# A pre-norm attention and MLP block on one core: key and value loads enter the DMA queue one attention step later, and two low parts go to GpSimd

## The chip, the cores and the metric

The kernel runs on one core of a Trainium2 chip. The metric is the device time of one execution in microseconds, the median of several runs. TensorE is PE in the profile, VectorE DVE, ScalarE ACT, GpSimd POOL, and SyncE SP. Almost all DMAs are issued by SP, so one queue, in one order, carries the loads, the stores and the transposes done by DMA.

## The reference, cut to what matters

```python
# x: (1, 2048, 512) float32; 32 heads of 16; window of 8 positions, 2 apart
def attention(x, wqkv, wo):
    q, k, v = split_heads(x @ wqkv)
    idx = pos[:, None] - 2 * arange(8)[None, :]          # masked where negative
    logits = einsum("bhsd,bhswd->bhsw", q, k[idx]) * Dh ** -0.5
    o = einsum("bhsw,bhswd->bhsd", softmax(where(idx >= 0, logits, -1e9)), v[idx])
    return merge_heads(o) @ wo

def mlp(x, w1, b1, w2, b2):                              # hidden width 1792
    return relu(x @ w1 + b1) ** 2 @ w2 + b2

h  = x + attention(layernorm(x), wqkv, wo)
h2 = h + mlp(layernorm(h), w1, b1, w2, b2)
```

## The kernel before, in words

All matrix products are made from float32 values split in two: a *high part* is the value rounded to a shorter float32 format by ACT (`hi`, L152), and a *low part* is the value minus its high part, a subtraction on DVE or POOL (`lo`, L155). Each product is three matmul passes, high by high, low by high, high by low. TensorE so does 2,414 matmuls, and the program's order is written so that they follow each other without a gap.

The 2,048 rows are 16 tiles of 128 positions. Tiles of even and of odd positions are kept apart, so the window with its stride of 2 becomes 8 neighbouring rows. The projections `q`, `k`, `v` are written to a DRAM buffer `qkv_d` and read back in windows.

*Attention* runs beside the matmuls, on DVE and POOL, and takes no matmul. It is a generator (`attention`) that hands out one *step* at a time. `dots(j)` multiplies a window of keys `k` with queries in PSUM, `qp` (L340, result `pr`); a reduction (L374) makes logits of it. `weigh(j)` multiplies a window of values `v` with the weights (L351, result `pr` too); POOL then adds the eight rows of the window in three instructions (`add_up`, L408), into `o`. Tiles `k`, `v` and `q` have two buffers each and `pr` three. Each step loads the key or value window of the step two ahead of it: `load_k`, and with every second one `load_q`, at the end of `dots`; `load_v` at the end of `weigh` (DMAs L247 and L260). The window so loaded goes into the buffer that the multiplication just emitted reads, so the DMA has to wait for that multiplication, and SP, which issues in order, waits with it. ACT copies `q` to PSUM (L268).

The order of everything is written by *slots*. A slot is one block of matmuls. What goes with a slot is put in lists: `due` (run at its end, before attention), `amid`, and `late` (after attention). `end_slot` runs `due`, then `pump`, which draws attention steps until their estimated DVE time has caught up with TensorE's, then `amid` and `late`. In the first pass over the MLP (4 tiles; u = 0) each slot also loads a block of `w2` (`raw`, L1057), splits it (ACT cast to `big_h`, low part `big_l` by POOL, every third by DVE), and stores the low part to DRAM for later passes (`stash`, `w2l_d`, L1086). The results `o` are turned to the layout that TensorE needs through 16-bit planes: ACT splits (`pl`, L621), a DMA transposes (L625), ACT joins (L630), then ACT rounds to the high part (`oh`, or `ohl` for every fourth tile) and DVE makes the low part. The product with `wo` reads these.

For the last four tiles the first MLP product is made from 7 instead of 8 block products, with sums of blocks of its input. `split_last` prepares them for tiles 14 and 15: `tr` is the joined tile `pl`; `hs_[1]` and `ls_[1]` are the high and low part of its second half; `sm[1]` and `sm[2]` are sums (in `s`), whose high and low parts follow. All of its subtractions and additions are on DVE.

Of the kernel before, what the change touches and what calls it, by code (L numbers as in the profile page):

```python
# [58 lines left out]
def block_kernel(ctx, tc, x, wqkv, wo, w1, b1, w2, b2, out):  # L59
    nc = tc.nc  # L60
# [75 lines left out]
    def dve(t):  # L136
        now["dve"] += t
# [16 lines left out]
    def lo(eng, dst, src, h):  # L154
        eng.tensor_tensor(out=dst, in0=src, in1=h, op=ALU.subtract)  # L155
# [86 lines left out]
    def load_window(n, j, c, name):  # L242
        s, g0, ng = items[n]
        u, b, e, i0 = where(s)
        t = att.tile([P, R + W - 1, GC], F32, name=name)
        sl = (R if u == 0 else RI) + W - 1
        nc.sync.dma_start(t[:, :sl], chain(e, g0 + j, c, CH // 2 * b + 1 + i0,  # L247
                                           [[R * GC, P], [GC, sl], [1, GC]]))
        return t
# [6 lines left out]
    def load_q(n, j):  # L256
        s, g0, ng = items[n]
        u, b, e, i0 = where(s)
        q = att.tile([P, 2, RI, GC], F32, name="q")
        nc.sync.dma_start(q.rearrange("p j i c -> p j (i c)"),  # L260
                          chain(e, g0 + j, 0, PAD + CH // 2 * b + i0,
                                [[R * GC, P], [CS, 2], [1, RI * GC]]))
        return q
# [7 lines left out]
    def attention():  # L271

        N = len(items)

        def ready(n):
            gps = [(items[n][1] + j) // 2 for j in range(0, items[n][2], 2)] if n < N else []
            return n < N and all((items[n][0] // RI, gp) in stored and gp in padded
                                 for gp in gps)

        steps = [(n, j) for n in range(N) for j in range(items[n][2])]  # L280
        ks, vs, qs, qps, ex = {}, {}, {}, {}, {}


        logits = psum.tile([P, 2, D // 2], F32, name="ex", tag="ex")

        def ahead(n, j, by):
            i = steps.index((n, j)) + by
            return steps[i] if i < len(steps) else (N, 0)

        def load_k(n, j):  # L290
            if ready(n) and (n, j) not in ks:
                ks[n, j] = ks[n - 1, j] if items[n][0] == 1 else load_window(n, j, 1, "k")
                if j % 2 == 0:
                    qs[n, j] = load_q(n, j)

        def load_v(n, j):
            if ready(n) and (n, j) not in vs:
                vs[n, j] = vs[n - 1, j] if items[n][0] == 1 else load_window(n, j, 2, "v")

        def next_q(n, j):  # L300
            if (n, j) in qs:
                qps[n, j] = q_to_psum(qs.pop((n, j)))

        while not ready(0):
            yield None
        for j in range(2):
            load_k(0, j)
        for j in range(2):
            load_v(0, j)
        for _ in range(DELAY):  # L310
            yield None
        for n in range(N + 1):

            new, old = n < N, n > 0
            while new and not ready(n):
                yield None
            ng = ng1 = 0
            if new:
                s, g0, ng = items[n]
                u, b, e, i0 = where(s)  # L320
                HG = ng * GH
                for j in range(2):
                    load_k(n, j)
                if (n, 0) not in qps:
                    next_q(n, 0)
                lf = logits[:, n % 2, :RI * W * HG].rearrange("p (i w h) -> p i w h", i=RI, w=W)
                mx = small.tile([P, RI, HG], F32, name="mx")
            if old:
                s1, g1, ng1 = items[n - 1]
                e1 = ex.pop(n - 1)  # L330
                sm = small.tile([P, RI, ng1 * GH], F32, name="sm")
                if s1 not in o_t:
                    o_t[s1] = att.tile([P, RI, D], F32, name="o", bufs=3)

            def dots(j):
                kwin = window(ks[n, j], s, [1, GC])
                pr = att.tile([P, RI, W, GH, DH], F32, name="pr", bufs=3)
                if j % 2 == 0:
                    qps["now"] = qps.pop((n, j))
                nc.vector.tensor_tensor(  # L340
                    out=pr.rearrange("p i w h d -> p i w (h d)"),
                    in0=qps["now"][:, j % 2].unsqueeze(2).to_broadcast([P, RI, W, GC]),
                    in1=kwin, op=ALU.mult)
                load_k(*ahead(n, j, 2))
                return pr

            def weigh(j):
                load_v(n - 1, j)
                vwin = window(vs[n - 1, j], s1, [DH, GH], [1, DH])
                p2 = att.tile([P, RI, W, GH, DH], F32, name="pr", bufs=3)  # L350
                nc.vector.tensor_tensor(  # L351
                    out=p2, in1=vwin, op=ALU.mult,
                    in0=e1[:, :, :, j * GH:(j + 1) * GH].unsqueeze(4).to_broadcast(
                        [P, RI, W, GH, DH]))
                sums.append((p2, o_t[s1], (g1 + j) * GC, s1))
                load_v(*ahead(n - 1, j, 2))

            for j in range(max(ng, ng1)):
                if j < ng:
                    pr = dots(j)  # L360
                    yield 1.22
                if old and j == 0:
                    nc.vector.tensor_reduce(out=sm, in_=e1.rearrange("p i w h -> p i h w"),
                                            axis=X, op=ALU.add)
                    yield 0.23 + 0.035 * ng1
                if 0 < j < ng1 or 0 < j == ng1 < ng:
                    if j == 1:
                        nc.vector.tensor_tensor(
                            out=e1, in0=e1, op=ALU.mult,
                            in1=sm.unsqueeze(2).to_broadcast([P, RI, W, ng1 * GH]))  # L370
                    weigh(j - 1)
                    yield 1.55 if j == 1 else 1.26
                if j < ng:
                    nc.vector.tensor_reduce(out=lf[:, :, :, j * GH:(j + 1) * GH], in_=pr, axis=X,  # L374
                                            op=ALU.add)
                    yield 1.22
                    if j % 2:
                        next_q(*((n, j + 1) if j + 1 < ng else (n + 1, 0)))
                if old and j == 0:
                    nc.vector.reciprocal(sm, sm)  # L380
                    yield 0.26
            if new and b == 0:
                nc.vector.tensor_tensor(
                    out=lf, in0=lf, op=ALU.add,
                    in1=mask[:, i0:i0 + RI].unsqueeze(3).to_broadcast([P, RI, W, HG]))
                yield 0.16 + 0.07 * ng
            if old and ng1 >= ng:
                weigh(ng1 - 1)
                yield 1.26
            if new:  # L390
                nc.vector.tensor_reduce(out=mx, in_=lf.rearrange("p i w h -> p i h w"), axis=X,
                                        op=ALU.max)
                nc.vector.tensor_tensor(out=lf, in0=lf, op=ALU.subtract,
                                        in1=mx.unsqueeze(2).to_broadcast([P, RI, W, HG]))
                ex[n] = lf
                yield 0.42 + 0.15 * ng
                nc.scalar.activation(lf, lf, AF.Exp, scale=DH ** -0.5)

    sums = []

    def add_up(p2, o, c0, s):
        w = W // 2
# [9 lines left out]
    def pump(until=None):  # L414

        while (done[until] < G) if until is not None else (now["dve"] < now["pe"]):
            if until is None and now["dve"] > now["pe"] - HALF:
                run(amid)
            todo = sums[:]
            sums.clear()  # L420
            t = next(stream, "end")
            for a in todo:
                add_up(*a)
            if t == "end":
                now["dve"] = 1e9
                return
            if t is None:
                now["dve"] = max(now["dve"], now["pe"])
                return
            dve(t * SLOW[min(now['sub'] + 1, 2)])  # L430
# [306 lines left out]
    def split_last(i, tr):  # L737
        hs_, ls_ = [a[:, :, i] for a in hh], [a[:, :, i] for a in hl]
# [4 lines left out]
        j = i - RI  # L743
# [12 lines left out]
        hi(hs_[1], tr[:, 2:])  # L756
        tt(out=sm[1], in0=tr[:, 2:], in1=a21, op=add)
        tt(out=sm[2], in0=sm[1], in1=tr0[:, :2], op=sub)
        lo(nc.vector, ls_[1], tr[:, 2:], hs_[1])
        hi(a_h[2][:, :, j], sm[2])  # L760
        lo(nc.vector, a_l[2][:, :, j], sm[2], a_h[2][:, :, j])
        if not j:
# [331 lines left out]
    for u in range(R - 1):  # L1094
# [11 lines left out]
        for i in js:  # L1106
            t = R * (u + 1) + i
            if not end:
                a = i // 2 if u == 2 else 0
# [148 lines left out]
```

## Time and profile before

| | |
|---|---|
| median of 3 runs | 504.54 us (503.73 to 505.6) |
| the profiled execution | 504.29 us, of which the span from first to last instruction is 502.5 us |
| granted TensorE clock | 1.000 |
| TensorE matmuls busy | 496.0 us, 99% of the span |
| DVE, ACT, POOL busy | 381.6 us (76%), 301.6 us (60%), 353.9 us (70%) |
| DMA | 103.15 MB, mean 205 GB/s |
| chain that ended last | PE 80%, DVE 5%, POOL 4%, ACT 4%, DMA 3%, issue 3% |

TensorE's busy time is nearly the whole span, so what counts is where it stops and what it then waits for. The other engines are idle a quarter to a third of the time, and a delay on one of them costs nothing until a matmul waits for it. The chain of waits follows the work that ended last back to its start.

### The profile page before, as it was taken

Reading aid. Unit: us, or ns where it says so; the run is one execution under the profiler, and the core shown is the slowest. Engines: PE = TensorE matmul, PEld = TensorE weight load, DVE = VectorE, ACT = ScalarE, POOL = GpSimd, SP = SyncE. Lnnn points to the kernel's source line nnn. Section 1 sums busy time; section 2 is a strip of 40 time slices with the busy share of each in tenths; the row PEclk is TensorE's granted clock in tenths of the full one; section 3 lists DMA queues with packets and bytes.
Section 4 is the critical chain, followed back from the end, with each engine's and each line's share of the span. In section 5 each row is a group of like instructions: output and inputs, shape, how many; then the busy total and the mean of one; then the engine's idle time right before and its main releaser. Section 6 shows DMA issues by size and latency. Waiting matters only on the chain.

```text
span 502.5 us, 7519 instructions
## 1 busy us (share of the span) xinstructions
PE 496.0 (99%) x2414; PEld 420.5 (84%) x2414; DVE 381.6 (76%) x524; ACT 301.6 (60%) x540; POOL 353.9 (70%) x430
## 2 busy tenths in 40 slices
PE   8999999999999999999999999999999999999997
PEld 7999888888888888887888888888888888998986
DVE  6479899988989899988879998888974155833233
ACT  4635687668446758368564555755554958766541
POOL 5714898885685999869777877769799363786610
PEclk9999999999999999999999999999999999999999
DMA  9679979889698989589676756966654566355112
GB/s 280 184 221 243 294 234 316 254 291 282 201 226 255 299 283 257 182 239 224 195 253 209 211 150 193 232 213 237 211 160 66 128 165 188 112 162 167 64 42 86
DMA packets 111472, 103.15 MB, mean 205 GB/s; under 512 B 31560, under 2 KB 79944, under 8 KB 111432
## 3 DMA queue, kind: packets, MB, share of 16 engines
q1 hardware_dynamic: 110488, 102.14, 69.5%
q10 hardware_dynamic: 944, 0.52, 0.3%
q8 instruction: 19, 0.31, 0.3%
q14 instruction: 21, 0.17, 0.1%
HBM read 72.65 MB, written 24.25 MB: 193 GB/s over the span
## 4 chain that ended last, share of the span: by engine, by line
PE 80%; DVE 5%; POOL 4%; ACT 4%; DMA 3%; issue 3%; ACTq 0%; SPq 0%; DVEq 0%; POOLq 0%
PE mm L228 41%; PE acc L899 23%; PE wo L228 8%; PE mm L822 7%; PE tr L201 2%; POOL pr L408 1%; DVE pr L351 1%; DMA raw<-in_B_w_dram 1%; DMA o<-pl 1%; DMA wraw<-in_A_wqkv_dram 1%; POOL rl L155 1%; DVE ex L374 1%; DVE pr L340 1%; ACT pl L621 1%; ACT big_h L152 1%
## 5 line engine op out<-in xcount | busy, mean ns | idle before, releaser
L408 POOL TENSOR_TENSOR pr<-pr 128x512 f32<-128x512 f32 (+1 forms) x128 | 134.2, 1049 | 36.7 <-DVE pr L351 31.4
L228 PE MATMUL mm<-big_l,w_h 128*128 128x512 f32 x336 | 88.5, 390 | 0.0
L351 DVE TENSOR_TENSOR pr<-ex,v 128x1024 f32<-128x1024 f32 x64 | 78.0, 1220 | 12.2 <-POOL o L408 8.0
L340 DVE TENSOR_TENSOR pr<-qp,k 128x1024 f32<-128x1024 f32 x64 | 76.8, 1200 | 11.7 <-ACT qp L268 7.9
L374 DVE TENSOR_REDUCE ex<-pr 128x64 f32<-128x1024 f32 x64 | 78.5, 1226 | 2.0
L228 PEld LDWEIGHTS mm<-big_l,w_h 128*128 128x128 f32 x336 | 62.9, 188 | 13.5 <-ACT r L875 0.2
L155 POOL TENSOR_TENSOR rl<-r,rh 128x512 fp32r<-128x512 f32 x42 | 54.7, 1306 | 25.5 <-ACT rh L152 25.4
L228 PE MATMUL mm<-big_l,xh 128*128 128x512 f32 (+1 forms) x208 | 55.8, 378 | 0.0
L228 PE MATMUL mm<-big_h,xh 128*128 128x512 f32 (+1 forms) x208 | 53.6, 378 | 0.9 <-ACT xh L152 0.8
L228 PE MATMUL mm<-big_h,xl 128*128 128x512 f32 (+1 forms) x208 | 52.6, 374 | 0.0
L899 PE MATMUL acc<-big_h,rh 128*128 128x512 f32 x190 | 52.0, 391 | 0.0
L899 PE MATMUL acc<-big_l,rh 128*128 128x512 f32 x190 | 52.0, 390 | 0.0
L899 PE MATMUL acc<-big_h,rl 128*128 128x512 f32 x190 | 51.7, 389 | 0.0
L228 PE MATMUL mm<-big_l,w_l 128*128 128x512 f32 x168 | 44.9, 389 | 0.0
L228 PEld LDWEIGHTS mm<-big_h,xh 128*128 128x128 f32 x208 | 37.7, 188 | 7.8 <-ACT xh L152 2.0
L228 PEld LDWEIGHTS mm<-big_h,xl 128*128 128x128 f32 x208 | 38.2, 188 | 6.0 <-DVE xl L155 0.2
L899 PEld LDWEIGHTS acc<-big_h,rl 128*128 128x128 f32 x190 | 35.7, 188 | 7.4
L899 PEld LDWEIGHTS acc<-big_l,rh 128*128 128x128 f32 x190 | 35.6, 188 | 7.5
L228 PEld LDWEIGHTS mm<-big_l,xh 128*128 128x128 f32 x208 | 37.5, 188 | 4.9
L899 PEld LDWEIGHTS acc<-big_h,rh 128*128 128x128 f32 x190 | 35.0, 188 | 6.7
L875 ACT ACTIVATE r<-mm,b_sb 128x512 f32<-128x512 f32 x42 | 28.7, 684 | 14.0 <-PE mm L228 13.1
L228 PEld LDWEIGHTS mm<-big_l,w_l 128*128 128x128 f32 x168 | 31.5, 188 | 6.6
(160 smaller groups left out, 910.6 us busy)
## 6 DMA issues: line engine op xcount, KB each, us to landing
k<-qkv_d SPq DMA_DIRECT2D x48, 288.0 KB, 3.6
v<-qkv_d SPq DMA_DIRECT2D x48, 288.0 KB, 3.7
qkv_d<-y SPq DMA_DIRECT2D x18, 512.0 KB, 4.0
big_l<-w2l_d SPq DMA_DIRECT2D x24, 256.0 KB, 3.2
xt<-in_A_x_dram SPq DMA_DIRECT2D x16, 256.0 KB, 4.3
q<-qkv_d SPq DMA_DIRECT2D x32, 128.0 KB, 3.7
h<-in_A_x_dram SPq DMA_DIRECT2D x16, 256.0 KB, 3.6
h_d<-h SPq DMA_DIRECT2D x16, 256.0 KB, 2.8
```

Source lines behind the costliest of these rows:

```text
L152: nc.scalar.copy(dst, src)
L155: eng.tensor_tensor(out=dst, in0=src, in1=h, op=ALU.subtract)
L201: nc.tensor.transpose(tr[:, k, :], src[:, k * P:(k + 1) * P], ident)
L228: nc.tensor.matmul(ps, l(k), r(k), start=(n == 0), stop=(n == 3 * KB - 1))
L340: nc.vector.tensor_tensor(out=pr.rearrange("p i w h d -> p i w (h d)"), in0=qps["now"][:, j % 2].unsqueeze(2).to_broadcast([P, RI, W, GC]) ...
L351: nc.vector.tensor_tensor(out=p2, in1=vwin, op=ALU.mult, in0=e1[:, :, :, j * GH:(j + 1) * GH].unsqueeze(4).to_broadcast([P, RI, W, GH, DH]))
L374: nc.vector.tensor_reduce(out=lf[:, :, :, j * GH:(j + 1) * GH], in_=pr, axis=X, op=ALU.add)
L408: nc.gpsimd.tensor_tensor(out=dst, in0=p2[:, :, :w], in1=p2[:, :, w:2 * w], op=ALU.add)
L621: nc.scalar.copy(two_planes(planes[key][1]), halves_of(src))
L822: nc.tensor.matmul(ps, sta[y][:, k], mov[x][:, k], start=(first and q == 0), stop=(last and q == len(terms) - 1), skip_group_check=True)
L875: nc.scalar.activation(r, ps, AF.Relu, bias=b1_sb[:, f:f + 1])
L899: nc.tensor.matmul(acc[j], l[:, j * P:(j + 1) * P], w[f], start=(first and n < len(js)), stop=(last and n >= len(terms) - len(js)))
```

## The change

The loads of a step are no longer issued at its end. They are put in a list, `loads`, and `pump` issues what is in the list right before it draws the next step. Within one `pump` call nothing but an `amid` chore can come between. But the last step of a `pump` leaves its loads in the list until the next `pump`: by then the `amid` and `late` chores of this slot and the `due` chores of the next have put their DMAs into the queue. Of the 112 loads of keys and values 35 change places with later DMAs, and 9 of the 32 loads of queries with them; at most six DMAs come ahead of one load. No instruction of PE or ACT changes place.

The second part moves the low part `ls_[1]` in `split_last` from DVE to POOL, for tiles 14 and 15.

```diff
@@ dots(j)
                     in1=kwin, op=ALU.mult)
-                load_k(*ahead(n, j, 2))
+                loads.append((load_k, ahead(n, j, 2)))
                 return pr
@@ weigh(j)
                 sums.append((p2, o_t[s1], (g1 + j) * GC, s1))
-                load_v(*ahead(n - 1, j, 2))
+                loads.append((load_v, ahead(n - 1, j, 2)))
@@
-    sums = []
+    sums, loads = [], []
@@ pump(until)
                 run(amid)
             todo = sums[:]
             sums.clear()
+            ready_loads = loads[:]
+            loads.clear()
+            for fn, a in ready_loads:
+                fn(*a)
             t = next(stream, "end")
@@ split_last(i, tr)
         tt(out=sm[2], in0=sm[1], in1=tr0[:, :2], op=sub)
-        lo(nc.vector, ls_[1], tr[:, 2:], hs_[1])
+        lo(nc.gpsimd, ls_[1], tr[:, 2:], hs_[1])
         hi(a_h[2][:, :, j], sm[2])
```

The first place is SP's queue in the first MLP pass, around the transpose of the first `o` tile of that pass. `raw` is a block of `w2`, `w2l_d` the store of a low part. Before:

```order
L247 DMA v<-qkv_d 128x576
L247 DMA k<-qkv_d 128x576
L260 DMA q<-qkv_d 128x2x128
L625 DMA_TRANSPOSE o<-pl 128x8x128
L1057 DMA raw_2307<-in_B_w_dram 128x512
L1086 DMA w2l_d<-big_l 128x512
L247 DMA k<-qkv_d 128x576
```

The same place of SP's queue after the change (lines below the diff are four higher):

```order
L247 DMA v<-qkv_d 128x576 x2
L629 DMA_TRANSPOSE o<-pl 128x8x128
L1061 DMA raw_2303<-in_B_w_dram 128x512
L1090 DMA w2l_d<-big_l 128x512
L247 DMA k<-qkv_d 128x576
L260 DMA q<-qkv_d 128x2x128
L247 DMA k<-qkv_d 128x576
```

A load of keys and one of queries moved behind the transpose, the block of `w2` and the store. The store waits for a low part of POOL.

The second place is DVE in `split_last` for tiles 14 and 15, before:

```order
L757 TENSOR_TENSOR s<-pl 128x2x128
L758 TENSOR_TENSOR s<-s,pl 128x2x128
L155 TENSOR_TENSOR big_l<-pl,big_l 128x2x128
L155 TENSOR_TENSOR big_l<-s,big_l 128x2x128
L757 TENSOR_TENSOR s<-pl 128x2x128
L758 TENSOR_TENSOR s<-s,pl 128x2x128
L155 TENSOR_TENSOR big_l<-pl,big_l 128x2x128
L155 TENSOR_TENSOR big_l<-s,big_l 128x2x128
L766 TENSOR_TENSOR s<-pl 128x2x128
```

And POOL at that time after the change:

```order
L683 TENSOR_TENSOR h<-h,b_sb 128x512
L155 TENSOR_TENSOR tl<-traw,th 128x512 x2
L155 TENSOR_TENSOR rl<-r,rh 128x512
L155 TENSOR_TENSOR big_l<-pl,big_l 128x2x128 x2
L155 TENSOR_TENSOR tl<-traw,th 128x512
L854 TENSOR_TENSOR r<-u,p 128x256
```

The two rows `big_l<-pl,big_l` left DVE's list, and stand on POOL behind `rl` and ahead of the next `tl`.

## The prediction

> **What bounds the kernel now.** I read the busy times by stretch first, since TensorE is busy for 496.0 of 502.5 us and the question is where the rest lies. Columns: stretch, its length, then busy time (and instructions) of PE, PEld (weight loads), DVE, ACT, POOL, the clock, the DMA share and GB/s.
>
> ```profile
> 17.00:227.00 210.00, 210.00 (x997) 178.10 (x996) 186.66 (x245) 130.24 (x261) 157.36 (x200) 1.00 0.84 251
> 227.00:230.00 3.00, 2.49 (x12) 1.74 (x11) 1.73 (x2) 2.97 (x5) 2.67 (x4) 1.00 1.02 231
> 230.00:426.00 196.00, 196.00 (x880) 162.29 (x879) 149.91 (x202) 118.38 (x187) 144.26 (x165) 1.00 0.68 190
> 426.00:432.00 6.00, 5.53 (x43) 5.00 (x42) 5.58 (x13) 4.16 (x8) 2.56 (x3) 1.00 0.06 17
> ```
>
> From 17 to 426 us, which is where all the moved loads lie, TensorE misses 0.51 us, in one place. Between 426 and 432 it misses 0.47, in the place of the second edit. The timeline of PE shows both (start, length, engine, line, operation; in brackets the idle time before and who ended it):
>
> ```profile
> 227.34 1.07 PE L899 MATMUL acc<-big_h,rl 128*128 128x512 f32 x4
> 228.91 1.20 PE L228 MATMUL wo<-wo_h,ohl 128*128 128x512 f32 x4 [0.51 <-ACT ohl L152]
> ...
> 426.64 0.40 PE L822 MATMUL mm<-wo_h,tl 128*128 128x256 f32 x2
> 427.50 0.51 PE L822 MATMUL mm<-wo_l,th 128*128 128x256 f32 x2 [0.47 <-DVE wo_l L155]
> ```
>
> The chain of waits says what the first stop hangs on (start, length, what):
>
> ```profile
> 202.43 1.30 POOL pr L408
> ...
> 218.33 1.05 ACT pl L621
> ...
> 228.24 0.63 ACT ohl L152
> 228.91 3.01 PE wo L228 x12
> 231.93 2.72 PE mm L228 x12
> ```
>
> POOL's sums from 202.43 give the `o` tile that ACT splits at 218.33, and ACT's `ohl` at 228.24 lets TensorE go on. What starts POOL later at 202.43 makes the stop longer.
>
> **The most that can be gained.** Twelve matmuls take 2.72 us in an even run, 0.227 each. The four from 227.34 would make room for the next at 228.25, so 0.66 us is lost by 228.91; the first twelve then take 3.01, another 0.29. The stop is worth 0.95 us in all, 0.44 over its idle time. The second, with the same surplus as an estimate, is worth 0.47 + 0.44 = 0.91. If both go, the sum is 1.86 us, 0.37%. A change of 0.5%, 2.5 us, is about what a measurement of this kernel can tell from none, so the change cannot make a difference on the fast side that a measurement shows; on the slow side nothing limits it so.
>
> **Edit 1, the loads.** No instruction is added or removed; 44 loads stand later in SP's queue and the DMAs that they let pass stand earlier. DVE's use of values and keys, and ACT's of the blocks of `w2` (idle time before each, and who ended it):
>
> ```profile
> L351 DVE TENSOR_TENSOR pr<-ex,v 128x1024 f32<-128x1024 f32 x64 | 78.0, 1220 | 12.2 <-POOL o L408 8.0 <-DMA v<-qkv_d 1.9
> L340 DVE TENSOR_TENSOR pr<-qp,k 128x1024 f32<-128x1024 f32 x64 | 76.8, 1200 | 11.7 <-ACT qp L268 7.9 <-POOL o L408 3.6
> L152 ACT CAST big_h<-raw 128x512 fp32r<-128x512 f32 x12 | 7.4, 616 | 2.4 <-DMA raw<-in_B_w_dram 2.4
> ```
>
> Loads hardly make DVE wait now: 1.9 us in 64 steps for values, none for keys. So most delays have cover, the time between landing and use. What passes ahead has little to give by itself either: ACT waited 2.4 us in all for the blocks of `w2`, while TensorE ran on. The transposes are the exception that could help the stop at 228.91. I look at the place where cover is thinnest, SP's queue at 190 us with what ACT and DVE do there, and POOL (its rows last):
>
> ```profile
> 190.86 0.32 SPq L247 DMA_DIRECT2D k<-qkv_d  x1
> 191.27 0.39 SPq L260 DMA_DIRECT2D q<-qkv_d  x1
> 191.75 1.24 SPq L625 DMA_TRANSPOSE o<-pl  x1
> 193.08 0.53 SPq L1057 DMA_DIRECT2D raw<-in_B_w_dram  x1
> 195.26 0.32 SPq L1086 DMA_DIRECT2D w2l_d<-big_l  x1
> 196.17 1.17 ACT L630 COPY pl<-o 128x1024 uint16<-128x1024 uint16 x1 [0.24 <-DMA o<-pl]
> 198.36 1.22 DVE L340 TENSOR_TENSOR pr<-qp,k 128x1024 f32<-128x1024 f32 x1
> 199.50 1.72 DVE L155 TENSOR_TENSOR ol<-pl,oh 128x512 fp32r<-128x512 f32 x1
> 193.93 1.29 POOL L155 TENSOR_TENSOR big_l<-raw,big_h 128x512 fp32r<-128x512 f32 x1
> 199.37 1.30 POOL L155 TENSOR_TENSOR rl<-r,rh 128x512 fp32r<-128x512 f32 x1
> ```
>
> *The gain side.* The transpose no longer stands behind the key load, which SP could only issue at 190.86 when DVE had freed its buffer, nor behind the query load; it goes 0.9 us earlier at the least (191.75 - 190.86), and more by what SP waited before 190.86. ACT waited 0.24 us for it at 196.17. Nothing follows from this: the `ol` that DVE makes of it at 199.50 already takes 1.72 us, because it ends only after POOL's `rl` (199.37 + 1.30 = 200.67). Gain taken: 0. Its far end is the whole first stop, 0.95.
>
> *The loss side.* The store `w2l_d` at 195.26 waits for POOL's low part (193.93 + 1.29 = 195.22), and the moved loads wait with it: keys at about 195.7, queries at about 196.1 (0.41 apart as now), instead of 190.86 and 191.27, 4.8 us later. DVE uses both at 198.36, through ACT's copy of the queries. How long a query load takes is shown once by a wait and once by the page's median (SP and ACT rows, then the page's row, last number: us to landing):
>
> ```profile
> 176.22 0.43 SPq L260 DMA_DIRECT2D q<-qkv_d  x1
> 178.97 0.38 ACT L268 COPY qp<-q 128x256 f32<-128x256 f32 x1 [3.72 <-DMA q<-qkv_d]
> q<-qkv_d SPq DMA_DIRECT2D x32, 128.0 KB, 3.7
> ```
>
> By the first, 2.75 us from issue to use, the copy starts at 198.9 and DVE's L340 at 199.3; by the second, at 199.8 and 200.2. L340 takes 1.22. In the first case `ol` is ready to run at 200.5, still under POOL's `rl`, and ends at 201.2 as before: POOL's start at 202.43 does not move, price 0. In the second `ol` starts at about 201.4, after `rl`. Without that wait it takes 0.69 at most (1.72 less the 1.17 from 199.50 to 200.67 leaves 0.55), so it ends at 202.1 instead of 201.22: 0.9 later, and with it POOL's chain, ACT and the stop at 228.91. So edit 1 costs 0 to 0.9. I take 0.1: the first case is the nearer row, a query load issued right behind a key load in the same stretch, and it leaves the path unmoved.
>
> Other places by the same reading: loads go behind such stores in the slots before this one too. From the issue at 190.86 to the use at 198.36 are 7.5 us, of which a load needs 2.75 to 3.7 by the rows above, so a delay up to 3.8 us is covered where the distances are like these. From 230 to 426 TensorE never stops. I take 0 there; a delay of DVE that reaches a matmul would cost its length.
>
> **Edit 2, two low parts by POOL.** DVE loses two instructions of 0.42 us. The question is what DVE was doing around them (DVE's rows, then ACT's, then POOL's):
>
> ```profile
> 421.28 1.10 DVE L757 TENSOR_TENSOR s<-pl 128x256 f32<-128x256 f32 x1 [3.52 <-POOL tl L155]
> 422.49 0.43 DVE L758 TENSOR_TENSOR s<-s,pl 128x256 f32<-128x256 f32 x1
> 422.83 0.42 DVE L155 TENSOR_TENSOR big_l<-pl,big_l 128x256 fp32r<-128x256 f32 x1
> 423.39 0.43 DVE L155 TENSOR_TENSOR big_l<-s,big_l 128x256 fp32r<-128x256 f32 x1
> 422.95 0.41 ACT L152 CAST big_l<-s 128x256 fp32r<-128x256 f32 x1 [0.36 <-DVE s L758]
> 424.64 0.41 ACT L152 CAST big_l<-s 128x256 fp32r<-128x256 f32 x1 [0.98 <-DVE s L758]
> 420.81 1.29 POOL L155 TENSOR_TENSOR rl<-r,rh 128x512 fp32r<-128x512 f32 x1
> 431.21 0.72 POOL L850 TENSOR_TENSOR r<-u,p 128x256 f32<-128x256 f32 x1
> ```
>
> The low part at 422.83 lies between L758, which ends at 422.92, and the low part of `s` at 423.39. That one needs ACT's cast, which waits for L758 and runs from 422.95 to 423.36. So the moved instruction fills a hole: without it DVE stands idle until 423.39 all the same. The second pair is alike, ACT's cast at 424.64 again waiting for DVE. Removing 0.84 us of DVE work therefore gains 0, and the stop at 427.50, which ends with a later DVE instruction of this chain, does not shrink. A gain is excluded by this as long as ACT's cast waits for L758.
>
> What it adds are two POOL instructions. POOL is free from 422.10 (420.81 + 1.29), and by the row at 431.21 a tensor of 128x256 takes it 0.72. But the row at 421.28 shows what the two engines do to each other: an instruction of DVE that takes 0.42 or 0.43 everywhere else here took 1.10, and ended 0.28 after POOL's `rl` did. Both inputs are in SBUF. If POOL's first low part starts when L758 ends, 422.92, it ends at 423.64. DVE's instruction of 423.39 then ends at 423.92 instead of 423.82, a loss of 0.1. The second low part has its input while DVE runs the next L757 and L758. If POOL comes in between these, L758 and all behind it are 0.72 later; if it comes behind them, into the hole of the next cast, the loss is as small as the first. Edit 2 so costs 0.1 + 0.1 to 0.1 + 0.72, 0.2 to 0.8, with 0 as the far end if the engines do not meet. I take 0.5, the middle, since I see no row that says which engine goes first. TensorE's stop at 427.50 grows by that; behind it TensorE is the bound until the end, so it shows in the time.
>
> [...]
>
> **The sum.** The profiled execution took 504.29 us, 0.25 below the median of the runs. 504.29 + 0.1 + 0.5 = 504.9.
>
> **The rivals.** *Late queries (slower).* The loads behind a store wait for POOL, DVE waits for the loads, POOL waits for DVE, and the next store waits for POOL. It decides when the copy of the queries starts later than 199.0, the last moment at which `ol` still ends under POOL's `rl`. At 0.9 for one such place, three places in a row (the stores of the slots at 172 to 196 us) give 2.7, and with edit 2 507.5. For it: POOL's row at 193.93 does set the store at 195.26, and a delay of 4.8 us is more than the cover of 3.8. Against it: 1.9 us of waiting for loads in all of the run before, so cover of several us at most places.
>
> *Both stops go (faster).* The earlier transpose and the queue that is no longer blocked let DVE run ahead, POOL reaches 202.43 a us sooner, and POOL's low parts fall in DVE's holes: 504.29 - 1.86 = 502.4. For it: the transpose feeds `ol` at 199.50, and DVE reaches the `pr` of 202.43 only behind that. Against it: ACT waited just 0.24 us for one, and edit 2 frees no DVE time that anyone waits for.
>
> *Nothing shows.* All moved loads have cover, what passes ahead has no one waiting for it, and POOL's low parts meet no DVE instruction: 504.3.
>
> **How the numbers follow.** Forecast 0.55; nothing shows 0.25; both stops go 0.12; late queries 0.08. The range goes from 503.0, part of the way to the case of both stops gone, to 506.6, which holds 0.9 and 0.8 together with some of the late queries; outside are most of the 0.08 and about 0.1 below. Faster by over 0.5% (under 502.0) is beyond the ceiling of the gain, and has only the spread of the runs for it: 0.04. Slower by over 0.5% (over 507.1) is the case of late queries, with a little left to the spread: 0.07. Within 0.5%: 0.89.
>
> **What would show it.** Right: PE idle by about 0.5 before `ohl` near 228.9, and by about 1.0 before `wo_l` near 428; DVE's rows near 422 to 425 with one of 0.7 to 1.1 us beside POOL's new ones; ACT's copy of queries near 198.9 ended by a DMA; the transpose issued before 190.9. Wrong: a stop of TensorE in a stretch that has none now; `ol` near 200 ending later than 201.5; the stop near 427.5 gone or smaller, which would mean that the freed DVE time was on the path after all.

## The result, and the profile after

The changed kernel took 508.38 us (median of 7 runs, 506.82 to 509.54) against 504.54 before (7 runs, 503.73 to 505.6). The ratio is 1.0069, 95% interval 1.0047 to 1.0092: slower, by 3.8 us in the medians. The forecast was 504.9 with a range to 506.6. The profiled execution took 507.16 us, its span is 505.3.

The page of the profile after, its head and busy times:

```profile
span 505.3 us, 7505 instructions
...
PE 496.3 (98%) x2414; PEld 420.5 (83%) x2414; DVE 380.3 (75%) x522; ACT 301.4 (60%) x540; POOL 355.9 (70%) x432
```

TensorE does the same work in the same time; only the span is longer. The busy times by stretch (columns as in the prediction), cut at the same two places, which now lie 2 us later:

```profile
17.00:228.00 211.00, 210.86 (x999) 178.50 (x998) 183.83 (x244) 129.36 (x259) 156.73 (x200) 1.00 0.83 250
228.00:232.00 4.00, 1.93 (x9) 1.26 (x9) 2.71 (x3) 3.90 (x7) 3.76 (x4) 1.00 0.91 217
232.00:428.00 196.00, 196.00 (x879) 162.29 (x878) 149.32 (x198) 118.20 (x188) 146.16 (x168) 1.00 0.66 189
428.00:434.00 6.00, 5.12 (x40) 4.60 (x38) 5.52 (x14) 3.70 (x8) 1.91 (x2) 1.00 0.10 29
```

TensorE misses 2.07 us in the second stretch, where it missed 0.51, and 0.88 in the last, where it missed 0.47. Its timeline shows both stops, with the same releasers as before:

```profile
228.05 1.07 PE L903 MATMUL acc<-big_h,rl 128*128 128x512 f32 x4
231.19 1.19 PE L228 MATMUL wo<-wo_h,ohl 128*128 128x512 f32 x4 [2.07 <-ACT ohl L152]
...
430.15 0.50 PE L826 MATMUL mm<-wo_l,th 128*128 128x256 f32 x2 [0.88 <-DVE wo_l L155]
```

The first stop is 1.56 us longer (2.07 - 0.51), the second 0.41 (0.88 - 0.47). Another 0.14 is missed ahead of 228 us. These are 2.1 of the span's 2.8; the rest is a few tenths at the start, near 63 us and at the end.

To see why `ohl` is late, follow the trace from the first MLP pass on. SP's issues, ACT, POOL and DVE of the changed kernel (start, length, engine, line, operation; in brackets the idle time before and who ended it):

```profile
173.95 0.43 SPq L599 DMA_DIRECT2D h<-in_A_x_dram  x1
174.47 2.45 SPq L247 DMA_DIRECT2D v<-qkv_d  x1
177.02 0.38 SPq L247 DMA_DIRECT2D k<-qkv_d  x1
177.45 0.42 SPq L260 DMA_DIRECT2D q<-qkv_d  x1
180.67 0.38 ACT L268 COPY qp<-q 128x256 f32<-128x256 f32 x1 [4.41 <-DMA q<-qkv_d]
182.94 0.62 ACT L152 CAST rh<-r 128x512 fp32r<-128x512 f32 x1
183.64 1.30 POOL L155 TENSOR_TENSOR rl<-r,rh 128x512 fp32r<-128x512 f32 x1 [1.11 <-ACT rh L152]
183.70 1.78 DVE L155 TENSOR_TENSOR big_l<-raw,big_h 128x512 fp32r<-128x512 f32 x1
195.67 1.30 POOL L155 TENSOR_TENSOR big_l<-raw,big_h 128x512 fp32r<-128x512 f32 x1
196.99 0.32 SPq L1090 DMA_DIRECT2D w2l_d<-big_l  x1
197.84 0.46 SPq L260 DMA_DIRECT2D q<-qkv_d  x1
201.15 0.38 ACT L268 COPY qp<-q 128x256 f32<-128x256 f32 x1 [0.39 <-DMA q<-qkv_d]
204.60 2.10 POOL L408 TENSOR_TENSOR pr<-pr 128x512 f32<-128x512 f32 x2 [1.87 <-DVE pr L351]
```

And the same two low parts, DVE's `big_l` and POOL's `rl`, in the kernel before:

```profile
181.65 0.83 DVE L155 TENSOR_TENSOR big_l<-raw,big_h 128x512 fp32r<-128x512 f32 x1
181.93 1.71 POOL L155 TENSOR_TENSOR rl<-r,rh 128x512 fp32r<-128x512 f32 x1
```

At 174 us a value load, which before was issued at the end of the step before this one, comes behind the load of `h` and right ahead of the key and query loads that the next `dots` needs. The copy of the queries starts at 180.67 against 178.97. In both traces ACT runs `big_h`, `r`, `r` and `rh` behind the copy, in this order, and the `rh` is late by as much as the copy (182.94 against 181.23, 1.71 us; the copy 1.70), and POOL, which had no idle time ahead of this `rl`, now waits 1.11 us. That `rl` then runs beside DVE's `big_l`. The two met in the kernel before as well, but there DVE's came first (181.65) and took 0.83 us, and POOL's took 1.71. Now POOL's comes first (183.64 against 183.70) and takes 1.30, and DVE's takes 1.78. From there all is late: `big_l` of POOL at 195.67 (before 193.93), the store at 196.99 (195.26), the queries behind it at 197.84 instead of 191.27, their copy at 201.15 (197.95), POOL's sums at 204.60 (202.43), and at the end `ohl`.

### The profile page after: what moved, and what is told of

Same layout as the page of the kernel before. It is cut to its first block, busy times and chain, and to the rows that moved or that the text cites. A ratio compares the mean times of both kernels' runs of the same rounds, so it can differ in the third digit from the quotient of the medians.

```text
span 505.3 us, 7505 instructions
## 1 busy us (share of the span) xinstructions
PE 496.3 (98%) x2414; PEld 420.5 (83%) x2414; DVE 380.3 (75%) x522; ACT 301.4 (60%) x540; POOL 355.9 (70%) x432
## 4 chain that ended last, share of the span: by engine, by line
PE 80%; DVE 2%; ACT 2%; POOL 2%; issue 1%; POOLq 0%; DVEq 0%; ACTq 0%
PE mm L228 36%; PE acc L903 26%; PE wo L228 9%; PE mm L826 7%; PE tr L201 2%; ACT pl L625 1%; POOL tl L155 1%; POOL pr L408 0%; DVE s L761 0%; PE half L926 0%; POOL rl L155 0%; DVE s L762 0%; ACT r L880 0%; POOL h L683 0%; DVE pr L351 0%
## 5 line engine op out<-in xcount | busy, mean ns | idle before, releaser
L340 DVE TENSOR_TENSOR pr<-qp,k 128x1024 f32<-128x1024 f32 x64 | 76.9, 1201 | 13.6 <-ACT qp L268 10.4
```

The lines of the kernel that those rows point to most:

```text
L340: nc.vector.tensor_tensor(out=pr.rearrange("p i w h d -> p i w (h d)"), in0=qps["now"][:, j % 2].unsqueeze(2).to_broadcast([P, RI, W, GC]) ...
```

## Experiments

Each kernel ran beside the kernel before on the same chip, whose medians were 504.0 to 504.58 us; ratios are to it.

### The two edits apart

The loads alone: the change, with

```diff
-        lo(nc.gpsimd, ls_[1], tr[:, 2:], hs_[1])
+        lo(nc.vector, ls_[1], tr[:, 2:], hs_[1])
```

> Only the deferred loads; the low part ls_[1] is on DVE again. Theory A (queries that are loaded behind a store that waits for POOL reach ACT late, ACT's queue delays POOL's rl and DVE's multiplication, POOL's sums start later, and TensorE waits longer for ohl near 230 us): the stop there stays at about 2.1 us against 0.5 before, the stop near 428 is 0.5 again, the span is 504.1 to 504.9 against 502.5, the ratio to before 1.003 to 1.005. Theory B (the loss comes of the two low parts on POOL): ratio 1.000, both stops as before. Theory C (the loss is the lower granted clock of some runs, not the stop): span of runs at clock 1.0 as before, and 2 us more where the clock is 0.996.

The low parts alone: the kernel before, with that line the other way round.

> Only the two low parts on POOL; the loads are issued at once as before. Theory A: the stop near 230 us is 0.5 as before, the one near 427 us 0.9 against 0.5, the span 502.9, the ratio 1.0008 (within the spread). Theory B: the ratio is that of the whole change, 1.005 to 1.007. Theory C: ratio 1.000 to 1.001, with a clock of 1.0 in all runs.

The loads alone: 506.84 us, ratio 1.0053 (1.0030 to 1.0075). The low parts alone: 504.78, 1.0005 (0.9994 to 1.0016). TensorE's waits in the first and then in the second (what, us in total, times, longest):

```profile
PE wo L228 <- ACT ohl L152: 2.1, 1, 2.1
...
PE mm L826 <- DVE wo_l L155: 0.5, 1, 0.5
```

```profile
PE mm L822 <- DVE wo_l L155: 0.9, 1, 0.9
```

Each edit lengthens its own stop and not the other's. In the profile of the low parts alone the first stop, 0.51 before, isn't there at all, though nothing ahead of it was changed: so it varies by half a microsecond from one execution to the next. Theory B is out. Of theory C something is left: in 5 of 9 runs the first kernel's clock was 0.992 to 0.997, and four runs at 0.999 or 1.0 had a median span of 504.1 (the kernel before beside it 502.8), the five others 506.4. That is taken up below.

### Which of the loads

The loads alone, but not in the first MLP pass:

```diff
-                loads.append((load_k, ahead(n, j, 2)))
+                if now["sub"] == 0:
+                    load_k(*ahead(n, j, 2))
+                else:
+                    loads.append((load_k, ahead(n, j, 2)))
```

(and the same for `load_v`).

> The deferred loads alone, but in the first pass over the MLP (about 170 to 230 us), where slots also load and store blocks of w2, the loads are issued at once as before. Theory A: the stop near 229 us is 0.5 again, no stop elsewhere, the ratio 0.999 to 1.001. If loads deferred elsewhere cost too: a stop at another place and a ratio of 1.002 or above.

Ratio 1.0000 (0.9992 to 1.0009). The loads deferred everywhere else cost nothing that this interval of 0.1% shows. The next two split the pass by time: from here on the first place is 174 to 177 us, and the second is 190 to 198 us, the part of SP's queue that the section on the change lists. They have other slots in that condition: `88 <= now["slot"] < 94` leaves only the second place deferred, `94 <= now["slot"] < 102` only the first.

> The deferred loads alone, but in the first MLP pass only from the slot of the second place on (the keys and queries behind the transpose and the store at 190 to 198 us); in the six slots ahead of it the loads are issued at once as before. By the prediction's own bounds for this place, 0 to 0.9 us: the copy of the queries starts at 198.9 to 199.8 and the stop near 229 us is 0.5 to 1.4, the ratio 1.000 to 1.002. If this place makes the whole loss by itself: the copy at 201, the stop 2, the ratio 1.004 to 1.006.

> The complement: in the first MLP pass the loads are deferred in its first six slots alone (the loads behind the store and the load of h at 174 to 177 us), and issued at once from the second place on. Theory A: the chain of POOL is 0.8 to 1.1 us late at 196 us, the keys and queries of the second place are in time, the stop is 1.0 to 1.4, the ratio 1.001 to 1.002; with the other run's surplus it adds up to the 1.6 us of both. By the prediction, which took 0 here: the stop 0.5, the ratio 1.000.

The second place alone: 1.0020 (1.0005 to 1.0034), the first alone 1.0061 (1.0040 to 1.0083). Rows of ACT, POOL and DVE, then TensorE's stop, with the second place alone:

```profile
179.24 0.38 ACT L268 COPY qp<-q 128x256 f32<-128x256 f32 x1 [4.90 <-DMA q<-qkv_d]
182.20 1.63 POOL L155 TENSOR_TENSOR rl<-r,rh 128x512 fp32r<-128x512 f32 x1
181.92 0.75 DVE L155 TENSOR_TENSOR big_l<-raw,big_h 128x512 fp32r<-128x512 f32 x1
199.20 0.38 ACT L268 COPY qp<-q 128x256 f32<-128x256 f32 x1 [1.31 <-DMA q<-qkv_d]
202.65 2.12 POOL L414 TENSOR_TENSOR pr<-pr 128x512 f32<-128x512 f32 x2 [1.78 <-DVE pr L354]
229.13 1.21 PE L228 MATMUL wo<-wo_h,ohl 128*128 128x512 f32 x4 [0.57 <-ACT ohl L152]
```

And with the first place alone:

```profile
174.78 1.49 SPq L260 DMA_DIRECT2D q<-qkv_d  x1
179.77 0.38 ACT L268 COPY qp<-q 128x256 f32<-128x256 f32 x1 [4.23 <-DMA q<-qkv_d]
182.74 1.30 POOL L155 TENSOR_TENSOR rl<-r,rh 128x512 fp32r<-128x512 f32 x1 [0.80 <-ACT rh L152]
181.97 1.22 DVE L354 TENSOR_TENSOR pr<-ex,v 128x1024 f32<-128x1024 f32 x1 [0.57 <-POOL o L414]
183.12 1.47 DVE L155 TENSOR_TENSOR big_l<-raw,big_h 128x512 fp32r<-128x512 f32 x1
199.77 0.37 ACT L268 COPY qp<-q 128x256 f32<-128x256 f32 x1
203.61 2.11 POOL L414 TENSOR_TENSOR pr<-pr 128x512 f32<-128x512 f32 x2 [1.76 <-DVE pr L354]
230.23 1.42 PE L228 MATMUL wo<-wo_h,ohl 128*128 128x512 f32 x4 [1.87 <-ACT ohl L152]
```

In its profile the second place behaves as the prediction priced it: the copy at 199.20, between its 198.9 and 199.8, POOL 0.2 later than before, the stop 0.57. That execution, 504.38 us, is the second fastest of its twelve; the median is 505.61, 1.4 above the kernel before, and where the others lost it no run shows. The first place, which the prediction took at 0, makes nearly the whole stop by itself. There a copy that is 0.5 us later (179.77 against 179.24) makes `rl` 0.5 later, and DVE's L354 waits another 0.57 for POOL; DVE's `big_l`, so 1.2 later, is now behind POOL's `rl` and takes 1.47 instead of 0.75, and DVE's next L340 starts 1.9 later (185.64 against 183.72). The expectation, a stop of 1.0 to 1.4 and a ratio of 1.001 to 1.002, was too low. The times do not add up: the first place alone costs about as much as both. The stops nearly do: 0.06 and 1.36 above the 0.51 of before are 1.4, and both together gave 1.56.

The query load of this kernel was issued earlier than before (174.78 against 176.22; the issue itself lasts to 176.27) and used later. A value load of 288 KB more stood ahead of it and of its key load. In the packed traces the last landing mark of the query load comes 0.35 to 0.44 us behind that of the key load ahead of it in all four kernels: 178.89 and 178.53 before, 179.69 and 179.33 here, 180.60 and 180.16 with the whole change, 181.27 and 180.92 with the values alone. So here the query load lands right behind the load ahead of it, whenever it was issued.

Three more kernels cut the chain at other points. Queries issued at once, only keys and values deferred (`load_k` no longer asks for those that were):

```diff
+        def ask_q(n, j):
+            if ready(n) and j % 2 == 0 and (n, j) not in asked:
+                asked.add((n, j))
+                qs[n, j] = load_q(n, j)
...
+                ask_q(*ahead(n, j, 2))
                 loads.append((load_k, ahead(n, j, 2)))
```

> Only the deferred loads, and of these only keys and values: the queries are issued at the end of the step as before (the first of the three late ones still comes behind a store, since its step is drawn at another moment). Theory A: the two later queries are ahead of their stores, so the feedback is broken after the first place; the copy that starts at 201.15 in the changed kernel starts at 198.5 to 200, the stop near 230 us is 0.5 to 1.3, the span 502.5 to 503.7, the ratio 1.000 to 1.0025. A variant, A2 (the late keys and values hold DVE as well): the stop stays at 2 us and the ratio at 1.003 to 1.005.

Only values deferred:

```diff
-                loads.append((load_k, ahead(n, j, 2)))
+                load_k(*ahead(n, j, 2))
```

> Of the deferred loads only those of values; keys and queries are issued at the end of the step as before, and the low part ls_[1] is on DVE. At the first place (174 to 177 us) the key and query loads still follow a value load and a load of h, but at the second (190 to 198) they are ahead of the transpose and the store again. Theory A: what makes the stop long is the second place's keys and queries; the copy of the queries near 198 us no longer waits for a DMA, the stop near 229 us is 0.5 to 1.0, no clock below 0.998, the ratio 1.000 to 1.002. If late values do it: the stop stays at 2, the ratio at 1.004 or above.

All deferred, and the store of the low part one slot later:

```diff
-            at(1, stash, f)
+            at(2, stash, f)
```

> All loads deferred as in the change, the low part ls_[1] on DVE, and the store of the low part of w2 put into the queue one slot later, so that its low part is made long before and SP need not wait for POOL in front of the loads. Theory A: the stop near 230 us falls from 2.1 to 0.5 to 0.9, the span is 502.5 to 503, the ratio 1.000 to 1.001. If what delays the loads is not the store's wait but the number of DMAs ahead of them (the block of w2, the transpose): the stop stays at 1.5 to 2 us, the ratio at 1.003 to 1.005.

Ratios 1.0017 (1.0006 to 1.0029), 1.0012 (1.0000 to 1.0024) and 1.0022 (1.0010 to 1.0034), with a stop of 1.1, 1.3 and 1.1 us. Each takes away roughly 60 to 80% of the loss of the loads alone and none all of it; the later store came out between its two expectations. The late queries, the late keys and the store in front of both are links of one chain; which of the loads at the first place weighs most, these runs don't settle: with the values alone the copy waited 7.24 us there, and the stop was still only 1.3.

### What a stop costs

The kernel before, with ACT's join and cast of that one tile repeated ahead of `ohl`, once each:

```diff
+        for _ in range(1 if t == 6 else 0):
+            nc.scalar.copy(...)         # the join of the o tile again
+        for _ in range(1 if t == 6 else 0):
+            hi_T(tr, [oT[t][0]])
```

> The kernel before, all loads in their old places; ACT repeats one join of the o tile and one cast of it (1.1 and 0.5 us, the same values written again) right before the ohl that TensorE waits for near 229 us, so that the stop there is 2.1 us long as in the changed kernel. If a stop costs just its length: every run at clock 1.0, span 504.2 to 504.4, the time 506.1, the ratio 1.003. If a stop of about 2 us also brings a stretch at half clock in some runs (in the run of the deferred loads alone, PE's clock reads 0.84, 0.50 and 0.87 in the 7 us behind the stop, 1.7 us of work lost): a part of the runs, some 3 to 7 of 12, shows a clock of 0.993 to 0.997 and is 1.7 us longer, the median 506.2 to 508, the ratio 1.004 to 1.006. If the low clock comes from the deferred loads and not from the stop: all at 1.0.

And with the join repeated twice:

```diff
-        for _ in range(1 if t == 6 else 0):
+        for _ in range(2 if t == 6 else 0):
             nc.scalar.copy(...)
```

> As the run with the stop alone, with one more repeated join: the stop near 229 us is 2.9 to 3.2 us. If a stop costs its length and the clock does not matter: 1.1 to 1.2 us more than that run, the median 508.2. If the share of runs with a lowered clock grows with the stop's length: all or nearly all runs at 0.993 to 0.998, the median 509 or more, the ratio 1.010 or above.

The first had a stop of 1.78 us, took 507.0 us and a ratio of 1.0071 (1.0052 to 1.0091): the loss of the whole change, with every load in its old place. The second had 2.97 us, took 511.41, ratio 1.0122 (1.0091 to 1.0154). The stops are 1.27 and 2.46 longer than before, the medians 3.0 and 7.0 us. How much of that is the stop itself shows where the same matmuls are followed through TensorE's timelines. The table has the starts of the last four matmuls ahead of the stop, of the four behind it, and of those that come 36 matmuls later:

| profile of | `acc<-big_h,rl` | `wo<-wo_h,ohl` | `wo<-wo_h,oh` | first to second | second to third |
|---|---|---|---|---|---|
| not in the first pass, no stop | 227.59 | 228.59 | 236.89 | 1.00 | 8.30 |
| the kernel before, stop 0.51 | 227.34 | 228.91 | 237.21 | 1.57 | 8.30 |
| stop alone, 1.78 | 227.97 | 230.82 | 239.14 | 2.85 | 8.32 |
| the whole change, 2.07 | 228.05 | 231.19 | 239.48 | 3.14 | 8.29 |
| first place alone, 1.87 | 227.29 | 230.23 | 240.15 | 2.94 | 9.92 |
| loads alone, 2.06 | 229.91 | 233.04 | 242.96 | 3.13 | 9.92 |
| longer stop, 2.97 | 227.74 | 231.78 | 241.69 | 4.04 | 9.91 |

In the first four the matmuls behind take 8.3 us whatever the stop was: it costs its length. In the last three they take 1.6 us more. The windows behind the stop show why; first the kernel with the first place alone, then the longer stop (PEclk is the third number from the end):

```profile
230.00:232.00 2.00, 1.77 (x6) 1.45 (x7) 1.79 (x2) 2.00 (x4) 1.92 (x2) 0.76 0.98 205
232.00:234.00 2.00, 2.00 (x6) 1.53 (x5) 1.93 (x2) 1.94 (x4) 1.92 (x4) 0.50 1.19 293
234.00:236.00 2.00, 2.00 (x9) 1.63 (x8) 1.09 (x2) 1.83 (x3) 1.92 (x3) 0.89 1.00 324
```

```profile
230.00:232.00 2.00, 0.23 (x1) 0.23 (x2) 0.25 (x1) 1.94 (x4) 1.92 (x3) 0.97 1.18 260
232.00:234.00 2.00, 2.00 (x6) 1.52 (x6) 2.00 (x3) 1.97 (x4) 0.91 (x2) 0.50 0.63 191
234.00:236.00 2.00, 2.00 (x8) 1.56 (x6) 0.99 (x1) 1.97 (x3) 1.33 (x2) 0.67 0.52 143
```

The granted clock reads 0.50 in the middle window of both. Lost are 2 x (0.24 + 0.50 + 0.11) = 1.7 us in the first and 2 x (0.03 + 0.50 + 0.33) = 1.7 in the second, which at half clock is a stretch of about 3.4 us behind the stop. It doesn't happen in every run, and the length alone doesn't decide it: the stretch is there behind 1.87 us in the first place alone, and not behind 2.07 in the profile of the whole change, where all windows read 1.00.

Of the executions without a trace only the mean clock is known. By the profiles, one such stretch makes it about 0.997 (1.7 us of 508.0 with the longer stop, whose mean is 0.997; with the first place alone the mean is 0.995). With stops up to 1.3 us (the kernel before and the seven with the low parts alone, the queries at once, values only, the later store in both kernels, not in the first pass, and the second place alone) 7 of 179 runs show a mean clock below 0.998. With stops of 1.8 to 2.1 us it is 13 of 23 in the three kernels with deferred loads (first place, loads alone, the whole change), but only 1 of 6 with the stop alone, fewer than expected. With 3.0 us, and every load in its old place, it is 5 of 6; so late loads are not needed for it. Nor does every lowered mean come from the stop: the profile of the loads alone (0.992) has a second stretch at half clock between 9 and 12.5 us (0.77, 0.50 and 0.88 in the windows of 2 us from 8 to 14).

For the whole change this gives a sum. The two stops cost 2.0 us (1.56 and 0.41). The three runs with a clock of 0.999 or 1.0 took 506.82 to 507.16, about 2.3 above before; the four at 0.995 to 0.997 took 508.38 to 509.54, and the median is one of these. The medians of the two made stops are not explained in full. With the longer one TensorE stops a second time, where it doesn't before (what, us in total, times, longest; it lies at 254.57 us):

```profile
PE mm L228 <- DVE big_l L155: 0.9, 1, 0.9
```

Of the stop alone five runs are at 0.999 or 1.0 and took 506.13 to 508.35. The profiled one of them, 506.18, lost 1.3 us at the stop; where the others lost more stays open.

### Taking the stop away

Three tries to show that all of the loss goes through this stop, or to win it and the second stop. The whole change with the product with `wo` behind the next block of MLP products:

```diff
+            behind = []
...
+                if fn is wo_product and a[0] == 6:
+                    behind.append(a)
+                    continue
...
             if p < FB:
                 mlp1(u, fs[p])
...
+                for a in behind:
+                    wo_product(*a)
...
```

> The whole change, and one edit: the product with wo for the tile whose ohl TensorE waits for stands behind the block of first MLP products of the same slot instead of ahead of it, 2.7 us of matmuls later. Theory A says that all of the loss but the 0.4 us of the two low parts comes through this one stop: it is gone (or below 0.1), no run has a lowered clock, the span is 502.3 to 503.2, the ratio 0.999 to 1.001. If the late loads delay other matmuls too, the loss comes back as a stop at another place and the ratio stays at 1.003 or above.

The whole change with ACT's join and `ohl` of that tile ahead of the hidden block's `r`, `r`, `rh` instead of behind:

```diff
+                if fn is at and a[1] is o_join and a[2] == 6:
+                    due.setdefault(now["slot"], []).insert(0, (o_join, (6,)))
+                    continue
```

> The whole change, and ACT makes the join of the o tile and its ohl before, instead of behind, the three instructions of the next hidden block (r, r, rh): 1.8 us earlier on ACT, nothing else moved (PE's order, which made the earlier trial with the later product slow through the shared PSUM buffers, stays). Theory A (all of the loss but the two low parts comes through this stop): the stop falls from 2.1 to 0.2 to 0.6, the runs have no lowered clock, the time is 504.3 to 505.2, the ratio 1.000 to 1.002. If the late loads cost elsewhere too, the ratio stays at 1.004 or above.

The kernel before with that, and in `split_last`:

```diff
         hi(a_h[1], s32[1])
+        lo(nc.vector, a_l[1], s32[1], a_h[1])
         for j in range(RI):
...
-        for m in (1, 3):
-            lo(nc.vector, a_l[m], s32[m], a_h[m])
+        lo(nc.vector, a_l[3], s32[3], a_h[3])
```

> The kernel before with two edits that leave the loads alone: the same order on ACT as in the run with the join first, and in split_last the low part of the first block sum ahead of DVE's four sums for the others. By the ceiling in the prediction both stops go, worth 1.86 us: the ratio 0.9963. If only the idle times count: 0.98 us, 0.998. If r and rh, which come later now, delay POOL's rl and the matmuls that read it: a new stop, 1.000 or above.

None did it: 512.68 us (1.0178, 1.0164 to 1.0192), 507.45 (1.0063, 1.0043 to 1.0082) and 505.51 (1.0024, 1.0011 to 1.0036). TensorE's waits, in this order:

```profile
PE wo L228 <- ACT r L879: 5.1, 2, 3.8
```

```profile
PE tr L201 <- ACT hn L196: 1.3, 1, 1.3
```

```profile
PE mm L822 <- ACT p L835: 1.5, 1, 1.5
PE tr L201 <- ACT hn L196: 1.4, 1, 1.4
```

In the first, `wo` shares its PSUM buffers with the MLP products ahead of it, and waits for ACT to read them. In the others `ohl` comes in time, but `hn` (near 250 us) and, in the last, `p` (near 431), which stand behind it on ACT, are late; in the second `wo` also still waits 0.7 us, now for `r`. Both stops of the kernel before did go in the last one, and two new ones took their place. So these runs don't show that the whole loss goes through the one stop. The timelines do for the profiled execution: the first matmuls behind the first stop start 2.28 us later than before (231.19 against 228.91), those behind the second 2.65 (430.15 against 427.50), and the second stop is 0.41 longer. Nothing between the two stops adds to the delay. The kernel before with the later product of the first try and the `split_last` of the third went the way of the first:

> The kernel before with two edits that leave the loads alone: the product with wo of that tile behind the block of MLP products, and in split_last the low part of the first block sum ahead of the four sums that DVE makes for the others. By the ceiling in the prediction, both stops go and with them 1.86 us: span 500.7 to 501, time 502.7, ratio 0.9963. If the idle times alone count and not the surplus of the matmuls behind them, 0.98 us: ratio 0.998. If the later product makes its follower late: a new stop near 240 us, ratio 1.000.

Ratio 1.0155 (1.0137 to 1.0173). Its profiled execution took 1,774 us, its four others 510.69 to 512.83, so no row of it is shown. Last, the kernel before with only `at(2, stash, f)` in place of `at(1, stash, f)`:

> The kernel before with one edit: the store of the low part of w2 one slot later, so that no load stands behind a store that waits for POOL. If that wait costs something before as well (a key load at 195.67 us stands right behind it), POOL's sums start a little earlier, the stop near 229 us is 0 to 0.4, the ratio 0.998 to 1.000. If it is hidden there: 1.000, the stop 0.5.

The stop fell to 0.2, the ratio is 0.9999 (0.9982 to 1.0017): nothing to measure. No version beat the kernel before.

## Why the prediction was wrong, and where it was right

**The step that failed** is "Other places by the same reading ... I take 0 there". I took one delay that is covered ("up to 3.8 us where the distances are like these") for all of them, and looked only at DVE's wait for loads. At 174 to 177 us the cover was gone already: the row of the copy that I quoted waits 3.72 us for its queries. A value load slipped in ahead, and the price came by way of ACT, in whose order the `rh` that POOL's `rl` reads stands behind the copy. The term measured 1.4 us of stop with this place alone (1.87 against 0.51) instead of 0.

**The second failed step** is what comes behind a stop. The sum priced a longer stop by its length and had no term for the clock. The length holds while the clock does: it is what the three runs at 0.999 or 1.0 show, 2.3 us in the median span (505.0 against 502.7), and that alone is more than the 0.6 forecast. The half clock behind the stop, 1.6 us where a trace shows it, takes the loss to the 3.8 of the medians.

**The most that can be gained** was put too high. It gave a stop a surplus of 0.44 for the matmuls behind it. In the two profiles where the first stop is missing (not in the first pass, and the low parts alone) the way from `acc` to `wo` takes 1.00 and 0.99 us instead of 1.57, and the 36 matmuls behind take 8.30 as before: the stop of 0.51 was worth 0.57, not 0.95. Differences well under the 0.5% that the prediction took as the least to be seen can be told, too; most of the intervals here are 0.1 to 0.2% to either side.

**Edit 1 at 190 to 203 us:** taken 0.1, between 0 and 0.9. In the profile with this place alone the copy, POOL's start and the stop came as priced, 0.06 of stop; the 1.4 us in the median of its runs stay open. In the changed kernel the copy was at 201.15, since the place inherits the delay of the first.

**The gain side:** 0 was right. The transpose was to go at least 0.9 us earlier than 191.75; with the second place alone it did (189.51), in the changed kernel it went at 192.36, and no one gained.

**Edit 2:** 0.5, measured 0.41, and 1.0005 for the edit alone. DVE and then POOL in the changed kernel:

```profile
425.97 0.42 DVE L761 TENSOR_TENSOR s<-pl 128x256 f32<-128x256 f32 x1
426.42 0.84 DVE L762 TENSOR_TENSOR s<-s,pl 128x256 f32<-128x256 f32 x1
...
425.98 1.00 POOL L155 TENSOR_TENSOR big_l<-pl,big_l 128x256 fp32r<-128x256 f32 x1 [0.22 <-ACT big_l L152]
```

POOL's second low part did come in between: it takes 1.00 us beside DVE's L761, and DVE's L762 takes 0.84, twice its 0.42. The first met no one on the path. The 0.72 taken for a low part that comes in between was too high: it held one instruction of DVE, for 0.42 us.

**The rival late queries** had the kind of mechanism: late loads, late POOL, late store, and the next loads. It left out the way by ACT's copy and `rh`, and its 507.5 against the 508.38 measured is in part luck: it has three places at 0.9 each, while the stop grew by 1.56, nearly all of it from one place, and the half clock is not in it. It had a chance of 0.08 because I asked only whether the last place would pass 199.0; it passes it by 0.2 us alone (199.20), and by more (201.15) when the first place has made POOL late.

## What to carry to other kernels

When a transfer is put behind others in one queue, look at every place where its user waits for it already, and at what stands behind that user on its engine: a copy that waits passes its delay on to work that has nothing to do with the transfer (here 1.70 us of the copy became 1.71 of `rh`). A delay that changes which of two engines' instructions comes first can grow on its way: here DVE's `big_l` took 1.47 us instead of 0.75, and 0.5 us became 1.9. And a stop of the engine that bounds the kernel has to be priced with what can follow it: its length at full clock, and here 1.6 us more when a stretch at half clock came behind it.

## What the runs showed of the hardware

With the first place alone TensorE's clock read 0.76, 0.50 and 0.89 in the three windows of 2 us behind a stop of 1.87 us, about 3.4 us at half, and 1.00 from 17 to 230 us and from 236 to 240. A lowered mean clock showed in 14 of 29 runs with stops of 1.8 to 2.1 us, and in 7 of 179 with stops up to 1.3 us. And the record of the clock is not complete. These are four matmuls of one kind at the start of the kernel before, then of the changed loads with the later store, and that kernel's window from 8 to 10 us:

```profile
8.00 0.86 PE L228 MATMUL mm<-big_h,xl 128*128 128x384 f32 x4
```

```profile
8.91 1.48 PE L228 MATMUL mm<-big_h,xl 128*128 128x384 f32 x4
```

```profile
8.00:10.00 2.00, 2.00 (x8) 1.99 (x7) 2.00 (x4) 0.23 (x1) 1.83 (x3) 1.00 1.12 329
```

The second four took 1.48 us instead of 0.86, at a clock that reads 1.00. In the packed traces the first entry of the clock lies at 5.43 us in the kernel before and at 10.85 in the other; ahead of the first entry the view prints 1.00 without a record. That the clock was lower there is an estimate from the 0.62 us (1.48 - 0.86) that these four lost; no entry shows it.

One DMA issue in this queue took 1.4 to 2.5 us where most take 0.3 to 0.5. It was a key load at 173.84 before (2.33 us), the value load at 174.47 with the whole change (2.45), the query load at 174.78 with the first place alone (1.49), and the key load at 174.81 with the values alone (1.45); whichever load stood there, its issue ended between 176.1 and 177.0. The runs do not show why.
